# A two-piece first copy, smaller first weight loads, another warm-up and another assumed landing time in a self-scheduling attention and MLP kernel

## The chip, the cores and the metric

The kernel runs on one core of a Trainium2 chip. The metric is the device time of one execution in microseconds (us). Before: 277.12 us, median of three executions (277.1 to 277.2). Several of the runs below were made on another chip or at another time, so each change is compared with executions of the kernel before in the same job, alternating with it on the same chip.

Short names: PE is the matmul engine, ACT, DVE and POOL are the other three compute engines, and SP is the queue that issues all DMAs. "PE idle" in this text is counted from starts: the distance from one matmul's start to the next one's, less the columns streamed at the full rate (a 512-column matmul follows the one before it after 0.216 us, a 320-column one after 0.136 us). The profile's own waits are about 0.17 us shorter, because it records 0.30 us for a 320-column matmul although the next one starts after 0.136 us.

## The reference, cut to what matters

```python
# x: 2048 tokens x 640; 32 heads of 20; MLP width 1536; all bf16
xn = layernorm(x)
q, k, v = split_heads(xn @ wqkv)
phi(u)  = concat(softmax(u @ w_phi), softmax(-(u @ w_phi)))     # per head
kv, z   = phi(k)^T v, sum over tokens of phi(k)
o       = (phi(q) @ kv) / (phi(q) @ z + 1e-6)
return x + o @ wo + (silu(xn @ w1) * (xn @ w3)) @ w2
```

The kernel folds w_phi into the query and key weights first ("the fold"). That needs wk transposed, and a transposing DMA load fetches it.

## The kernel before

The kernel is written for a builder inside the same file. The author gives nine streams of work (layer norm, folds, attention, MLP chunks and so on). The builder keeps a small model of each engine and of the DMA bus, and again and again places the step that the model says could start first. **The model's numbers decide the order of the instructions on the chip.** A wrong number costs nothing by itself, but it may give a worse order, and a corrected one may too.

```python
# in commit(): the model's time at which a DMA has landed
self.bus = max(self.bus, t + 0.5) + o.cost / (280e3 if o.part else 305e3)
o.end = self.bus + (1.6 if t < 3.5 else 2.6)
...
def mm(o, l, r, start, stop, shared=False, cost=None):
    ... cost=max(n / 2400 + 0.003, 0.055) if cost is None else cost
...
def first_loads():
    load_x(0, 1); load_x(1, 2); load_x(2, 3)            # token tiles of 128
    for a in (0, 320):                                  # wv in two halves
        P.dma("SP", wv[:, :, a:a + 320], ...)
    load_x(3, 4)
    w13(0, 512)                                         # w1, w3: first 512 columns = 4 MLP chunks
    P.dma("SP", phi_s[:], phi_t)
    P.dma("SP", wqkT[:, DC:2 * DC, :], A_wqkv[:, D:2 * D], True)   # wk, transposed
    load_x(4, 8); load_x(8, 12)
...
def warm_up():                                          # PE works on zeros until tokens are there
    for _ in range(7):
        mm(bank(7), z[:, 0:128], z, True, True)         # 512 columns
    for n, cols, rep in ((2, 88, 10), (4, 66, 8)):      # 52 small ones, row groups side by side
        ...
def xn_transpose(t, k):                                 # tiles 0 to 3: by PE, then a copy out of PSUM
    for dc in range(DC):
        tr(PSb[...], x_tok[:, t, 128 * dc:128 * dc + 128])
    evac(xnT[:, :, t * 128:(t + 1) * 128], src)         # one copy of 640 columns
...
def loads():                                            # tiles 4 to 15: normalised, then transposed by DMA
    ...  P.dma("SP", xnT[:, :, t * 128:(t + 1) * 128], x_tok[:, t, :], True)
    ...  # after tile 7: w13(512, 1024), load_x(12, 16)
def consts_late():                                      # at the end of the norm stream
    ...
    memset("POOL", v2[...][:, :, :, DH], 1.0)           # the ones beside v, interleaved with v's columns
...
# out_tile(), last tile: (0, 0, 384), (1, 384, D)
```

Until w13(512, 1024) has landed there are four MLP chunks (2.16 us of PE each) that PE can use. And the memset of v's ones writes between v's columns: the builder tracks memory in small pieces and finds both in the same ones, so it makes a v copy that is placed after the memset wait for it.

The softmax here doesn't subtract the row's maximum and nothing guards it: scores larger than these inputs give would overflow.

## Time and profile before

| | before |
|---|---|
| median time | 277.12 us |
| span of the profiled execution | 274.9 us |
| PE busy | 268.9 us |
| PE starts real work (first transposes) | 5.99 us |
| start of the last DVE add | 272.45 us |

Two lines of the page of the kernel before: the span, and each engine's busy time, share and instructions.

```profile
span 274.9 us, 4782 instructions
...
PE 268.9 (98%) x1961; PEld 163.3 (59%) x1961; DVE 181.9 (66%) x318; ACT 108.1 (39%) x197; POOL 60.5 (22%) x93
```

The waits of PE (us in total, how often, the longest in us):

```profile
PE PS L101 <- DVE t L101: 1.3, 1, 1.3
PE PS L101 <- ACT xnT L101: 1.0, 2, 0.8
PE PS L101 <- DVE x_tok L101: 0.6, 1, 0.6
PE PS L101 <- DMA wqkT<-in_A_wqkv_dram: 0.5, 1, 0.5
```

These four are all. The first is the time before anything is in SBUF. The others lie between 5 and 17 us. The opening in order of time (start, length, instruction, count, and in brackets the idle time before it and what ended it):

```profile
5.99 0.45 PE L101 MATMUL PS<-ident,x_tok 128*128 128x128 bf16 x5 [0.57 <-DVE x_tok L101]
6.48 0.70 ACT L101 ACTIVATE xnT<-PS 128x640 bf16<-128x640 bf16 x1 [4.17 <-PE PS L101]
7.24 0.85 PE L101 MATMUL PS<-wv,xnT 128*128 128x320 bf16 x5 [0.80 <-ACT xnT L101]
...
9.39 0.39 DVE L101 TENSOR_SCALAR x_tok<-x_tok,mv,rstd 128x640 bf16<-128x640 bf16 x1
9.90 0.44 PE L101 MATMUL PS<-ident,x_tok 128*128 128x128 bf16 x5
...
14.02 2.32 PE L101 MATMUL PS<-xnT,w_s 128*128 128x512 bf16 x10
16.79 1.76 PE L101 MATMUL PS<-BDc,wqkT 128*128 128x140 bf16 x30 [0.45 <-DMA wqkT<-in_A_wqkv_dram]
```

PE transposes tile 0 at 5.99 us, ACT copies it, the first v matmuls run at 7.24 us. The first MLP chunk runs at 14.02 us, then PE stands until wk's transposed load lands, folds at 16.79 us and runs the second chunk. The fourth chunk of the first 512 columns runs much later, as PE's own timeline shows:

```profile
39.28 2.32 PE L101 MATMUL PS<-xnT,w_s 128*128 128x512 bf16 x10
```

The end: DVE's last add, on the second part (256 columns) of the last tile:

```profile
272.45 0.42 DVE L101 TENSOR_TENSOR xres<-PS,xres 128x256 bf16<-128x256 f32 x1 [1.30 <-PE PS L101]
```

About 2.5 us pass from that add's start to the end.

### The profile page before, as it was taken

What the parts mean: (1) busy time and instruction counts of PE and PEld (TensorE: products, weight loads), DVE (VectorE), ACT (ScalarE), POOL (GpSimd) and SP (SyncE); (2) the same over time, 40 slices, a digit from 0 to 9 for tenths busy, and PEclk for the clock granted to TensorE, in tenths of its full rate; (3) what the DMA queues carried; (4) which work ended last, traced back from release to release, by engine and by line L of the source; (5) the groups of instructions that cost most, each with busy time, mean ns of one, the idle gap of its engine ahead of it and who ended that gap; (6) DMA issues with size and microseconds to landing.
All of it is one profiled execution on the core that took longest, in us unless ns stands there. A gap on an engine that the chain in (4) does not pass through costs nothing.

```text
span 274.9 us, 4782 instructions
## 1 busy us (share of the span) xinstructions
PE 268.9 (98%) x1961; PEld 163.3 (59%) x1961; DVE 181.9 (66%) x318; ACT 108.1 (39%) x197; POOL 60.5 (22%) x93
## 2 busy tenths in 40 slices
PE   6999999999999999999999999999999999999996
PEld 2656666676447555555555455567446777777774
DVE  5459869999764698999899799978963121111112
ACT  2567987987821335445554544411320000000000
POOL 4404493999984100000000000000000000000000
DMA  7971899650000731111112111232300212121211
GB/s 202 296 223 37 176 244 295 115 145 0 0 0 2 222 117 24 25 24 26 24 31 43 24 25 26 49 46 52 93 5 0 89 56 82 61 84 61 81 42 48
DMA packets 40326, 21.96 MB, mean 80 GB/s; under 512 B 26736, under 2 KB 40304, under 8 KB 40304
## 3 DMA queue, kind: packets, MB, share of 16 engines
q1 hardware_dynamic: 40304, 21.66, 31.9%
q8 instruction: 15, 0.25, 0.4%
q14 instruction: 7, 0.06, 0.1%
HBM read 12.81 MB, written 2.62 MB: 56 GB/s over the span
## 4 chain that ended last, share of the span: by engine, by line
PE 81%; DMA 7%; DVE 5%; SPq 2%; ACT 2%; issue 1%; POOL 1%
PE PS L101 81%; DMA wqkT<-in_A_wqkv_dram 4%; DVE bst L101 3%; DMA x_tok<-in_A_x_dram 3%; SPq L113 2%; ACT x_tok L101 1%; DVE mv L101 1%; POOL rstd L101 1%; ACT ekt L101 0%; DVE Wkp L101 0%; DVE hT L101 0%; DVE t L101 0%; ACT v L101 0%; DVE xres L101 0%; DVE x_tok L101 0%
## 5 line engine op out<-in xcount | busy, mean ns | idle before, releaser
L101 PE MATMUL PS<-xnT,w_s 128*128 128x512 bf16 x480 | 107.2, 379 | 0.1
L101 PEld LDWEIGHTS PS<-xnT,w_s 128*128 128x128 bf16 x480 | 46.8, 98 | 55.1 <-ACT Wkp L101 0.3
L101 PE MATMUL PS<-w_s,hT 128*128 128x320 bf16 (+2 forms) x384 | 54.9, 299 | 0.0
L101 DVE TENSOR_TENSOR xres<-PS,xres 128x640 bf16<-128x640 f32 (+2 forms) x17 | 13.4, 786 | 54.0 <-PE PS L101 54.0
L101 ACT ACTIVATE th<-PS 128x512 f32<-128x512 f32 x48 | 28.7, 598 | 46.8 <-PE PS L101 46.8
L101 PEld LDWEIGHTS PS<-w_s,hT 128*128 128x128 bf16 x384 | 37.6, 98 | 14.6
L101 DVE SCALAR_TENSOR_TENSOR t<-th,PS 128x512 bf16<-128x512 f32 x48 | 32.7, 682 | 15.4 <-ACT th L101 15.4
L101 POOL TENSOR_TENSOR ekt<-ekt,rS 128x640 bf16<-128x640 bf16 x32 | 39.4, 1271 | 4.1 <-DVE rS L101 4.1
L101 DVE SCALAR_TENSOR_TENSOR hT<-t,PS 128x512 bf16<-128x512 bf16 x48 | 33.0, 687 | 1.7
L101 PE MATMUL PS<-wv,xnT 128*128 128x320 bf16 x160 | 24.7, 299 | 1.0 <-ACT xnT L101 1.0
L101 ACT ACTIVATE EqT<-PS 128x512 bf16<-128x512 f32 x40 | 21.7, 595 | 9.9 <-PE PS L101 9.9
L101 PE MATMUL PS<-wo_s,oT 128*128 128x320 bf16 (+2 forms) x160 | 24.5, 299 | 0.0
L101 DVE TENSOR_TENSOR prod<-PS,g_s 128x1280 bf16<-128x1280 f32 x16 | 23.9, 1491 | 0.5
L101 PE MATMUL PS<-Wkp,xnT 128*128 128x320 bf16 x160 | 23.9, 299 | 0.1
L101 PE MATMUL PS<-xnT,Wqp 128*128 128x512 bf16 x100 | 23.7, 379 | 0.0
L101 ACT ACTIVATE ekt<-PS 128x640 bf16<-128x640 f32 x32 | 20.8, 717 | 6.0 <-PE PS L101 6.0
L101 DVE TENSOR_REDUCE S<-ekt 128x64 f32<-128x1280 bf16 x16 | 23.0, 1441 | 0.0
L101 PEld LDWEIGHTS PS<-wv,xnT 128*128 128x128 bf16 x160 | 15.2, 98 | 7.5 <-ACT xnT L101 1.5
L101 PEld LDWEIGHTS PS<-Wkp,xnT 128*128 128x128 bf16 x160 | 15.4, 98 | 6.4 <-ACT ekt L101 0.3
L101 PEld LDWEIGHTS PS<-wo_s,oT 128*128 128x128 bf16 x160 | 15.6, 98 | 6.1
L101 DVE BATCH_NORM_STATS2 bst<-x_tok 128x6 f32<-128x320 bf16 x32 | 15.3, 478 | 5.8 <-DMA x_tok<-in_A_x_dram 5.2
L101 ACT ACTIVATE e_s<-PS 128x64 f32<-128x64 f32 x32 | 9.1, 283 | 22.0 <-PE PS L101 21.0
(53 smaller groups left out, 162.4 us busy)
## 6 DMA issues: line engine op xcount, KB each, us to landing
w_s<-in_B_w_dram SPq DMA_DIRECT2D x6, 640.0 KB, 6.7
xres<-in_A_x_dram SPq DMA_DIRECT2D x16, 160.0 KB, 2.4
out_dram<-xres SPq DMA_DIRECT2D x15, 160.0 KB, 1.8
x_tok<-in_A_x_dram SPq DMA_DIRECT2D x3, 640.0 KB, 6.2
w_s<-in_B_w_dram SPq DMA_DIRECT2D x1, 1920.0 KB, 8.0
wv<-in_A_wqkv_dram SPq DMA_DIRECT2D x2, 400.0 KB, 4.6
wo_s<-in_A_wo_dram SPq DMA_DIRECT2D x1, 800.0 KB, 4.7
x_tok<-in_A_x_dram SPq DMA_DIRECT2D x4, 160.0 KB, 2.9
```

What stands on the lines that cost most here:

```text
L101: o = _Op(eng, lambda: m(*args, **kw), r, w, cost)
L113: o = _Op(eng, lambda: m(out, in_), self.regions(in_), self.regions(out), nbytes, True)
```

## The change

Its intent: let the first v matmuls start on a part of the first tile, load the first MLP columns in smaller pieces, tell the builder that wk comes 1 us later so that it puts other work before the fold, make the matmul costs truer, simplify the warm-up, and shorten the last add.

```diff
-                o.end = self.bus + (1.6 if t < 3.5 else 2.6)
+                o.end = self.bus + (1.6 if t < 3.5 else 2.6) + (o.part == "T" and o.cost > 4e5)
...
-             cost=max(n / 2400 + 0.003, 0.055) if cost is None else cost)
+             cost=n / 2400 + 0.0027 if cost is None else cost)
...                                   # tr(): cost 0.06 -> 0.056
-        w13(0, 512)
+        w13(0, 256)
+        w13(256, 512)
...                                   # warm_up()
-        for _ in range(7):
+        for _ in range(9):
             mm(bank(7), z[:, 0:128], z, True, True)
-        for n, cols, rep in ((2, 88, 10), (4, 66, 8)):
-            ...                       # the 52 small matmuls
...                                   # xn_transpose()
-        evac(xnT[:, :, t * 128:(t + 1) * 128], src)
+        if t == 0:
+            copy("ACT", dst[:, 0:2, :], src[:, 0:2, :])
+            copy("ACT", dst[:, 2:DC, :], src[:, 2:DC, :])
+        else:
+            evac(dst, src)
...                                   # out_tile(), last tile
-            for q, lo, hi in ((0, 0, 384), (1, 384, D)):
+            for q, lo, hi in ((0, 0, 512), (1, 512, D)):
```

Only the two large transposed weight loads are over 4e5 bytes, so the extra 1 us touches only them.

More of the change, by code (lines that the diff above doesn't have):

```diff
@@ L349, in mm @@
              dict(start=start, stop=stop, skip_group_check=shared),
-             cost=max(n / 2400 + 0.003, 0.055) if cost is None else cost)
+             cost=n / 2400 + 0.0027 if cost is None else cost)
     def tr(o, i, idn=None):
         idn = ident[:] if idn is None else idn
-        P.op("PE", "transpose", [o], [i, idn], (o, i, idn), cost=0.06)
+        P.op("PE", "transpose", [o], [i, idn], (o, i, idn), cost=0.056)
     def free(ap):
@@ L467, in warm_up @@
         memset("DVE", z, 0.0)
-        for _ in range(7):
+        for _ in range(9):
             mm(bank(7), z[:, 0:128], z, True, True)
-        for n, cols, rep in ((2, 88, 10), (4, 66, 8)):
-            r = 128 // n
-            for _ in range(rep):
-                for i in range(n):
-                    mm(bank(i, cols), z[r * i:r * i + r, 0:128], z[r * i:r * i + r, 0:cols], True, True,
-                       cost=0.05 / n)
     def xn_transpose(t, k):
@@ L481, in xn_transpose @@
         src = PSb[:, k * 1024:k * 1024 + D].rearrange("p (c n) -> p c n", n=128)
-        evac(xnT[:, :, t * 128:(t + 1) * 128], src)
+        dst = xnT[:, :, t * 128:(t + 1) * 128]
+        if t == 0:
[3 more added lines that the diff above has]
+            evac(dst, src)
     def block_diag():
```

## The prediction

> **What bounds the kernel now.** TensorE. The page gives PE 268.9 us busy of a 274.9 us span; the list of waits has only 3.6 us of PE waits, all in the first 17 us: 1.3 us (nothing loaded yet), 0.57 us for the first normalised token tile, 0.8 and 0.17 us for an ACT copy of a transposed tile, and 0.45 us for the transposed wk weights. From 17 to 272.45 us the timeline shows PE without a gap worth naming. About 2.5 us follow PE's last start (DVE add 0.42 us, store about 1.5 us). So the change can gain only in the opening gaps and in the tail: at most about 2 us, under 1%.
>
> **What the change does.**
>
> 1. First tile's copy in two pieces. ACT takes 0.70 us for 640 columns and 0.44 us for 320, so by that line (an estimate) 0.39 and 0.49 us for 256 and 384. The first two matmuls of the tile need only the first piece; the last three start about 0.15 us earlier. The next transposes are bound by DVE (tile 2 is normalised at 9.78 us, PE transposes it at 9.90), so I keep only 0.07 us.
>
> 2. wk transpose assumed later, by 1 us. This changes only the order in which the kernel's builder places work. PE now does one MLP chunk (14.02 to 16.2 us), stands until 16.79 us for wk's transposed load, folds wk, then does the next chunk. I expect two chunks (2.16 us each) before the fold; PE then reaches it near 18.3 us. Gain: the 0.45 us wait plus the drain, 0.6 us.
>
> 3. 256-column loads. Two more DMA issues (0.43 to 0.9 us each on the SP queue) and 512-byte rows. wk's transpose is issued at about 7.5 us, not 6.25, and lands 0.5 to 1.3 us later, at 17.2 to 18.0 us. Point 2 hides that. The load of tokens 4 to 7 (issued at 13.18 us) slips by about 1 us too; PE has one spare MLP chunk (run at 39.28 us before) to cover it. No gain by itself.
>
> 4. Warm-up: nine full matmuls instead of seven and 52 small ones. It ends near 5.2 us, not 5.42, so the gap before 5.99 us grows at no cost, if the clock stays up. The Trainium skill ("TensorE: Matmul & The Clock Gate", Part 1) says that the array runs at half rate until one window of about 3.4 us has been busy; here the warm-up matmuls are 0.43 us apart and the transposes at 5.99 us 0.056 us apart, so it agrees. I give 8% to a cold start.
>
> 5. Last tile 512 and 128. PE time is equal: at 128 columns the transposes go 0.056 us apart with a weight load each (the same page, "Back-to-back issue gap", says about 81 ns; this trace is faster). The last add shrinks from 0.42 to about 0.29 us (estimate from 0.82, 0.56 and 0.42 us for 640, 384 and 256 columns). The store has 256-byte rows; I expect the same 1.5 us. Gain 0.13 us.
>
> 6. Matmul costs in the builder become truer; the order may shift anywhere, worth plus or minus 0.3 us.
>
> Sum: 0.07 + 0.6 + 0.13 = 0.8 us: 276.3 us, range 275.6 to 277.1. Faster by over 2%: 0.01; within 2%: 0.97; slower: 0.02.
>
> **Shown right by:** no PE wait for wk's load and two MLP chunks before the fold; two ACT copies for tile 0; last add 0.29 us. **Shown wrong by:** PE still waiting for wk, the first real matmuls over 0.2 us apart, or new PE waits between 20 and 50 us for token tiles.
>
> **What would break it:** wk landing after 18.3 us, later token loads starving PE, or a cold clock.

## The result, and the profile after

The changed kernel took 277.65 us (median of six, 277.08 to 278.49); the kernel before, in the same job, 277.16 us (six, 277.02 to 277.33). The ratio is 1.002, with a 95% interval of 1.0004 to 1.0036. Ratios here are the mean time of one kernel's fast runs over that of the other's of the same rounds, so not quite the ratio of the medians quoted. The predicted 276.3 us and its range (to 277.1) were missed: a small gain was forecast and a small loss came.

The profiled execution is the fastest of the six. The same two lines of its page:

```profile
span 275.4 us, 4682 instructions
...
PE 269.4 (98%) x1911; PEld 161.9 (59%) x1911; DVE 182.0 (66%) x319; ACT 107.0 (39%) x197; POOL 60.5 (22%) x93
```

PE is as full as before, but 0.5 us more of it. PE's waits:

```profile
PE PS L101 <- DVE t L101: 1.3, 1, 1.3
PE PS L101 <- DVE x_tok L101: 1.0, 2, 0.6
PE PS L101 <- ACT xnT L101: 0.5, 1, 0.5
PE PS L101 <- ACT v L101: 0.3, 1, 0.3
PE PS L101 <- DMA xnT<-x_tok: 0.3, 1, 0.3
PE PS L101 <- ACT Wkp L101: 0.2, 1, 0.2
```

The wait for wk is gone. Three small ones have come: for ACT's copy of v, for a token tile's DMA transpose, and for a copy within the fold. The opening:

```profile
5.90 0.46 PE L101 MATMUL PS<-ident,x_tok 128*128 128x128 bf16 x5 [0.59 <-DVE x_tok L101]
6.39 0.76 ACT L101 ACTIVATE xnT<-PS 128x256 bf16<-128x256 bf16 x2 [4.09 <-PE PS L101]
6.83 0.96 PE L101 MATMUL PS<-wv,xnT 128*128 128x320 bf16 x5 [0.48 <-ACT xnT L101]
...
9.69 0.39 DVE L101 TENSOR_SCALAR x_tok<-x_tok,mv,rstd 128x640 bf16<-128x640 bf16 x1
10.14 0.45 PE L101 MATMUL PS<-ident,x_tok 128*128 128x128 bf16 x5 [0.37 <-DVE x_tok L101]
...
14.27 4.48 PE L101 MATMUL PS<-xnT,w_s 128*128 128x512 bf16 x20
18.58 1.11 PE L101 MATMUL PS<-BDc,wqkT 128*128 128x140 bf16 x18
...
28.09 2.32 PE L101 MATMUL PS<-xnT,w_s 128*128 128x512 bf16 x10
```

Two MLP chunks (20 matmuls) now stand before the fold, as predicted; the fold starts at 18.58 us with no wait for wk. All four chunks are used up by 30.25 us: the fourth, which ran at 39.28 us before, now runs at 28.09 us. The later fold delays more than itself. Tiles 4 and later are normalised, then transposed by DMA. ACT normalises tile 4 after the two exponentials of the first key tile (`ekt`), and these wait for PE's key matmuls, which follow the fold. ACT before (first two lines) and after:

```profile
22.38 1.30 ACT L101 ACTIVATE ekt<-PS 128x640 bf16<-128x640 f32 x2 [1.84 <-PE PS L101]
23.57 1.73 ACT L101 ACTIVATE x_tok<-x_tok,rstd 128x640 bf16<-128x640 bf16 x2
24.21 1.30 ACT L101 ACTIVATE ekt<-PS 128x640 bf16<-128x640 f32 x2 [1.54 <-PE PS L101]
25.40 1.73 ACT L101 ACTIVATE x_tok<-x_tok,rstd 128x640 bf16<-128x640 bf16 x2
```

So the first DMA transpose of a token tile is issued at 26.35 us, not 24.51. In all 16 profiles of fast executions it is issued 7.72 to 7.76 us after the fold starts. PE further on, at the two new waits:

```profile
39.76 1.52 PE L101 MATMUL PS<-wv,xnT 128*128 128x320 bf16 x10
41.56 1.52 PE L101 MATMUL PS<-Wkp,xnT 128*128 128x320 bf16 x10 [0.28 <-DMA xnT<-x_tok]
...
56.02 1.52 PE L101 MATMUL PS<-wv,xnT 128*128 128x320 bf16 x10
57.85 0.49 PE L101 MATMUL PS<-BDc,wqkT 128*128 128x140 bf16 x6 [0.32 <-ACT v L101]
```

The ten matmuls at 39.76 us need 1.36 us; the next start is 1.80 us later, so PE idles 0.44 us, for tile 8: its DMA transpose landed at 41.43 us, before at 40.80, when PE was still at its fourth chunk. Likewise 0.47 us before 57.85 us. What held the second, as ACT's and POOL's timelines show it (ACT's v copy, then POOL's memset of v's ones):

```profile
57.09 0.71 ACT L101 ACTIVATE v<-PS 128x640 bf16<-128x640 f32 x1 [2.61 <-POOL v L101]
54.62 2.37 POOL L101 MEMSET v<- 128x512 bf16 x1
```

The memset ends at 56.99 us and the copy starts at 57.09 us. In the kernel before, the same memset ran at 82.1 us, after all v copies. The end:

```profile
273.09 0.29 DVE L101 TENSOR_TENSOR xres<-PS,xres 128x128 bf16<-128x128 f32 x1 [0.26 <-PE PS L101]
```

The last add takes 0.29 us, not 0.42.

Counted from PE's first transposes (5.99 and 5.90 us) to PE's last matmul (272.14 and 272.84 us), the changed kernel needs 0.79 us more. From PE's starts, before against after:

| stretch | PE idle before | PE idle after | difference |
|---|---|---|---|
| first transposes to first MLP chunk (whole length 8.03, 8.37) | | | +0.34 |
| before the fold | 0.61 | 0 | -0.61 |
| in and just after the fold | 0.27 | 0.33 | +0.06 |
| near 41 us (token tile) | 0 | 0.45 | +0.45 |
| near 50 and 57 us (v copy, fold of the queries) | 0.24 | 0.75 | +0.51 |
| sum | | | +0.75 |

After that nothing more is won or lost: at 78 us ACT's instructions come 0.63 us later than before, and DVE's last add 0.64 us.

### The profile page after: what moved, and what is told of

It reads as the page before. It is cut to its first block, busy times and chain, and to the rows that moved or that the text cites. A ratio compares the mean times of both kernels' runs of the same rounds, so it can differ in the third digit from the quotient of the medians.

```text
span 275.4 us, 4682 instructions
## 1 busy us (share of the span) xinstructions
PE 269.4 (98%) x1911; PEld 161.9 (59%) x1911; DVE 182.0 (66%) x319; ACT 107.0 (39%) x197; POOL 60.5 (22%) x93
## 4 chain that ended last, share of the span: by engine, by line
PE 83%; DVE 5%; DMA 5%; POOL 3%; SPq 2%; issue 1%; ACT 1%; POOLq 0%; ACTq 0%
PE PS L101 83%; DMA x_tok<-in_A_x_dram 5%; DVE bst L101 3%; POOL ekt L101 2%; SPq L113 2%; POOL v L101 1%; DVE mv L101 1%; DVE S L101 1%; POOL eps L101 0%; ACT Wkp L101 0%; ACT v L101 0%; DVE hT L101 0%; DVE t L101 0%; DVE x_tok L101 0%; ACT Wqp L101 0%
## 5 line engine op out<-in xcount | busy, mean ns | idle before, releaser
L101 DVE BATCH_NORM_STATS2 bst<-x_tok 128x6 f32<-128x320 bf16 x32 | 15.3, 478 | 4.5 <-DMA x_tok<-in_A_x_dram 3.9
```

The costliest lines, as they stand in the source:

```text
L101: o = _Op(eng, lambda: m(*args, **kw), r, w, cost)
```

## The experiments

First theory ("the order"): what the reordering saves before the fold is lost again at 41 and 57 us. Rivals: the smaller loads cost; the new warm-up starts the clock late in some executions, which would explain the spread of 1.4 us. A third theory, the instruction refill, came from the first four runs.

Every edit is against the kernel before or the changed one, as said. I compared the instruction order of each edited kernel with that of its base. The two-piece copy, the small loads and the tail leave the order of PE, DVE and POOL as it is; the later wk alone decides the number of chunks before the fold and the place of the memset. The new warm-up changes the PE order only after 90 us. The traces show that such late changes of order cost nothing: the lead of that run over the kernel before is 0.70 us at 64 us and 0.69 us at the last add, and that of the changed kernel without the later wk (below) 0.74 us at both.

### One part alone on the kernel before

**Two-piece copy** (edit: the `xn_transpose` hunk).

> The kernel before with the first tile's copy in two pieces, and nothing else; the order of work on PE, DVE and POOL stays as before. If the copy is only a small local gain, as predicted, the first v matmul starts about 0.35 us earlier and the whole runs 0.1 to 0.3 us faster. If DVE's order (statistics of tile 3, which wait for their load, ahead of tile 2's normalisation) swallows it, under 0.1 us is left: PE stands longer before the transposes of tile 2.

Measured: 276.8 us against 276.71, ratio 0.9994 (0.9958 to 1.0031). Too wide to see 0.1 us. The profiled execution was an unlucky one in two ways: the first half of wv landed at 7.28 us instead of 6.34, which alone held the first v matmul to 7.41 us; and the array's clock fell back to half for one stretch. The profile by windows (length, busy us of each engine, then the clock as PEclk, DMA share, GB/s):

```profile
core 0: us, PE busy (x) PEld busy (x) DVE busy (x) ACT busy (x) POOL busy (x), PEclk, DMA share, GB/s
7.50:10.90 3.40, 3.40 (x17) 2.14 (x17) 1.51 (x4) 1.30 (x3) 0.95 (x3) 0.50 1.08 352
10.90:13.00 2.10, 2.10 (x20) 1.42 (x19) 0.84 (x2) 1.17 (x3) 0.48 (x1) 0.99 1.37 151
```

In that stretch 320-column matmuls started 0.267 us apart, not 0.136. So the part alone is inconclusive in time. That it moves the wait is seen in the changed kernel: first v matmul at 6.83 us, but 0.53 us of PE idle before tile 2's transposes, which there was none of before; tile 2's normalisation (9.69 us) stands behind tile 3's statistics on DVE.

**Small loads** (edit: the `w13` hunk), run twice.

> The kernel before with the first MLP columns in four 256-column loads instead of two of 512; the order of all engines stays as before. Loads theory: the wk transpose lands 0.5 to 2 us later, so PE's wait before the fold grows from 0.6 us to 1.1 to 2.6 us, tile 3 lands about 0.3 us later, and the run is 0.5 to 2 us slower, with a wider spread. Rival (the loads are harmless, the lost time is the order's): within 0.2 us of before.

Measured: 278.0 us against 276.71, ratio 1.003 (0.9994 to 1.0066). All six executions lie above 277.3. The profile had a cold clock until 10.47 us, so it could not say why.

> The small loads alone once more. Refill theory: the instruction packet falls between 12 and 15 us, amid the loads of w1, w3 or wk; wk lands at 16.7 us or later, PE stands 0.4 us or more before the fold, and the median is again 0.5 to 1.4 us above before. Rival (the first run was an unlucky chain of late clock starts): within 0.3 us of before.

Measured: 277.31 us against 276.8, ratio 1.0022 (1.0009 to 1.0035). With the clock up, wk landed at 17.09 us and PE idled 0.96 us before the fold. The instruction packet of the refill theory came at 12.4 us. So the small loads on the old warm-up do cost, here 0.5 us.

**New warm-up** (edit: the `warm_up` hunk).

> The kernel before with nine full warm-up matmuls in place of seven and 52 small ones. Warm-up theory: in some executions the clock is released later, so the median rises by about 0.5 us and the spread from 0.3 to over 1 us, as the changed kernel shows. Rival: no difference over 0.1 us and a spread of about 0.3 us.

Measured: 276.03 us against 276.71, ratio 0.9973 (0.9939 to 1.0008). Five of the 11 executions of before exceed 276.8, and two of this one's six; its four best lie at 275.9 to 276.06. So neither expectation held: it is 0.7 us **faster** in the medians, but the interval includes 1, so the times alone do not show it. Its trace shows no wait for wk at all: wk landed at 15.17 us, not 16.66.

**Later wk** (edit: the first hunk).

> The kernel before, but its builder assumes the two large transposes 1 us later; two MLP chunks then stand before the fold, and the POOL memset of v's ones moves to before the last v copies. Order theory: the 0.6 us wait for wk goes, but 0.3 to 0.5 us of PE idle come back near 41 us (a token tile's transpose, no MLP chunk left as filler) and about 0.5 us near 57 us (ACT's v copy waits for the memset): from 0.2 us faster to 0.4 us slower in all. If the order is not to blame, it runs 0.5 to 0.6 us faster.

Measured: 277.74 us against 276.71, ratio 1.0032 (0.9998 to 1.0067). The waits of PE in this profile that before does not have:

```profile
PE PS L101 <- DMA xnT<-x_tok: 0.7, 1, 0.7
PE PS L101 <- ACT v L101: 0.6, 1, 0.6
PE PS L101 <- ACT Wkp L101: 0.2, 1, 0.2
```

This one number in the model brings all three new waits of the changed kernel. Counted from starts, PE idles 0.86 us at 41 us and 0.76 us at 58 us. The order theory expected at most 0.4 us of loss; the medians say 1.0 us (the interval just includes 1).

### Why the new warm-up makes wk land earlier

Where the 52 small matmuls had been, 50 matmuls and as many weight loads are missing. The trace has, besides the data queue, a queue of kind "instruction": 15 packets of 16,384 bytes, spread over the whole span, one for every 124 matmuls on average (93 to 164). The 3,922 PE instructions in the profile of the kernel before, at the 64 bytes that the Trainium skill gives for one ("TensorE: Matmul & The Clock Gate", Part 2, step 2), make 15.3 such packets. The skill's page "Runtime: NRT & Kernel Launch", section "Instruction fetch mechanics", says that each engine's instruction store is refilled by DMA in blocks of 16 KiB, 256 instructions, and that the cost is mostly hidden. The size agrees. For PE itself it is hidden too: PE has no idle time at the later packets, at 28.11 and 61.02 us for example. The guess was that the packet holds up data that the DMA engines move at the same time.

Kernel before, DMA queues from 14.4 to 15.6 us (packets, MB, share; the data queue's line is left out), then the view of the transposed weight's tile: the load's time from issue (at 6.25 us) to landing, and PE's wait for it.

```profile
q8 instruction: 1, 0.02, 5.8%
DMA to landing us min/median/max: 10.4/10.4/10.4
  PE PS L101: 0.5, 1
```

Kernel before with the new warm-up, the same two views (load issued at 6.34 us); the data queue is the only one in this window. Its first instruction packet comes at 18.88 us, when wk has long landed, and PE has no wait for wk:

```profile
q1 hardware_dynamic: 225, 0.16, 81.9%
DMA to landing us min/median/max: 8.8/8.8/8.8
```

In all profiles of kernels with the old warm-up and 512-column loads (four, with the tail run below) the packet falls at 14.4 to 15.2 us, and wk lands 4.3 us after the small phi load ahead of it in the queue. In the nine where it falls later (from 18.7 us), wk lands 2.7 to 2.8 us after phi. (In the two with the old warm-up and small loads it falls before wk; see below.) To test this rather than argue it, I put 50 tiny matmuls back where PE stands idle anyway:

```diff
 # kernel before with the new warm-up; xn_transpose(), after tile 0's transposes
+        if t == 0:
+            z = t1[:, 2, :]
+            for n, cols, rep in ((2, 88, 9), (4, 66, 8)):
+                ...                   # 18 + 32 matmuls on zeros, into banks 4 to 7
```

> The kernel before with nine warm-up matmuls (the run that was 0.7 us faster) and 50 tiny matmuls on zeros put back, but in PE's idle stretch after the first tile's transposes (6.2 to 7.2 us), where they cost PE nothing. Refill theory: what delayed wk before was one 16 KB packet of PE's own instructions, at 14.4 us, amid wk's transposed load; with nearly as many PE instructions as before it falls there again, wk lands 4.3 us after the small phi load instead of 2.7, near 16.7 us, and PE again stands 0.3 to 0.7 us before the fold. Rival (nine full matmuls help by an earlier clock): wk lands near 15.3 us and PE does not wait for it.

Measured: 276.8 us against 276.68, ratio 1.001 (0.9989 to 1.0031): no gain over before is left, though this interval overlaps that of the new warm-up alone. The same two views, the queues from 14.7 to 16 us:

```profile
q8 instruction: 1, 0.02, 5.3%
DMA to landing us min/median/max: 10.3/10.3/10.3
  PE PS L101: 0.4, 1
```

The packet is back (14.81 us), wk lands at 17.01 us, 4.30 us after phi, and PE idles 0.53 us before the fold. The refill theory is shown: adding or removing 50 matmuls moves the packet, and wk with it by 1.5 to 1.8 us. The semaphore records of the traces show how. A load's completion is counted in 16 steps. In the kernel before, wk's last data packet ends at 14.65 us; 15 of the 16 steps come by 15.14 us and the last one at 16.66. With the new warm-up the last data packet ends at 14.65 us too, and all 16 steps come by 15.17 us. In all five profiles with the packet amid wk, one step alone is late, 2.19 to 2.25 us after the packet's start; the packet itself takes 1.05 to 1.11 us. So one of the 16 steps is held up, not the bulk of the data. Why that step comes another 1.1 to 1.2 us after the packet's end is not shown.

The small loads with the new warm-up:

> The small loads with the nine-matmul warm-up. Refill theory: the packet falls at about 19 us, wk lands at 15.6 to 16.2 us, PE waits at most 0.2 us for it, and the median is 0.3 to 0.8 us under before, as with the nine-matmul warm-up alone. Rival (the loads cost by themselves): 0.3 to 1 us above before.

Measured: 276.46 us against 276.8, ratio 0.9991 (0.9975 to 1.0008); packet at 18.93 us, wk landed at 15.75 us, no wait for wk. So the small loads are slow only together with the old warm-up: the packet then delayed the last of the four loads (in the repeat it landed 2.7 us after the third, where the others are 1.1 us apart), and wk after it.

### Parts of the changed kernel

> The changed kernel once more, beside the three below on one chip. If the order is what costs, the trace again has no PE wait for wk, two MLP chunks before the fold, and PE idle of 0.4 to 0.9 us near 41 us (a token tile's transpose) and of 0.5 to 0.8 us near 57 us (ACT's v copy behind the POOL memset). Median 0 to 1.2 us above before; spread over 0.5 us if loads and clock start vary.

Measured: 276.77 to 278.43 us in five executions against 277.08, ratio 1.0018 (0.9998 to 1.0038). The sixth, the profiled one, took 406.49 us at a granted clock of 0.658; it is not used, so the expected waits could not be checked here. The times agree with the first result.

**Memset late.** Edit on the changed kernel:

```diff
+        while done["n"] < T - 1:
+            yield None
         yield consts_late
```

> The changed kernel with the POOL memset of v's ones put late (after the 15th key tile's normalisation), where the kernel before has it; the PE order up to the key-value sums stays as in the changed kernel. Order theory: the idle near 57 us (0.5 to 0.8 us) goes and the run is 0.4 to 0.8 us faster than the changed kernel; the idle near 41 us stays. Rival (the time goes elsewhere, PE only waits later): under 0.2 us.

Measured: 276.73 us, ratio to before 0.9992 (0.9977 to 1.0008), beside 1.0018 for the changed kernel in the same job: 0.26%, or 0.7 us, as expected, though the two intervals overlap. The idle time at 57 us is gone, that at 41 us (0.60 us here) is not, although the clock started late in the profiled execution. In the trace the order theory's second half holds.

**An extra chunk at hand.** Edit, on top of the memset: w13(512, 640) after tile 5, the rest after tile 7.

> As the run before it, and 128 more columns of w1 and w3 are loaded earlier (after token tile 5's transpose is issued), so that one more MLP chunk is at hand near 41 us. If the chunk moved ahead of the fold was PE's filler for 41 us, the idle there goes, and the run is 0.4 to 0.8 us faster than the one with the late memset alone. If the builder does not place the chunk there (its PE order came out the same), or the extra loads delay the token transposes, the idle stays and nothing is gained.

Measured: 277.55 us, ratio 1.0011 (0.9991 to 1.003). A miss: the builder put no chunk there, and the two extra loads stand before the token transposes on the SP queue (tile 8's issued at 35.44 us instead of 34.12), so PE's idle time at 41 us grew from 0.60 to 1.11 us. It shows what PE waits for at 41 us, but not that a chunk there would cure it; that stays open.

**Without the later wk.** Edit: the first hunk undone in the changed kernel.

> The changed kernel without the assumption that wk lands 1 us later: one MLP chunk before the fold, the memset late by the builder's own choice. If the reordering is what costs, the waits near 41 and 57 us go (0.9 to 1.4 us of PE idle) and a wait for wk of at most 0.6 us comes, since wk lands at 15.7 to 16.2 us and PE reaches the fold near 16.4: 0.3 to 1.0 us faster than the changed kernel. If the later wk was needed, PE stands over 0.6 us before the fold.

Measured: 276.28 us against 276.68, ratio 0.998 (0.9963 to 0.9998). All waits of PE:

```profile
PE PS L101 <- DVE t L101: 1.3, 1, 1.3
PE PS L101 <- ACT xnT L101: 0.6, 2, 0.5
PE PS L101 <- DVE x_tok L101: 0.6, 1, 0.6
PE PS L101 <- ACT Wkp L101: 0.2, 1, 0.2
```

No wait for wk, although only one chunk stands before the fold: wk landed at 15.79 us and PE came at 16.24. No wait for a token tile or for v. Two groups remain (275.66 to 275.87 and 276.69 to 276.8). Against the changed kernel's 1.0018 and 1.002 (other jobs, each beside the kernel before) this is 0.4%, about 1.1 us, from one number of the model. It is the deciding run.

**With 512-column loads.** Edit: the `w13` hunk undone in the changed kernel.

> The changed kernel with its first MLP columns in two 512-column loads again; the order of all engines stays. If the four smaller loads cost (the wk transpose issued at 6.3 instead of 9.4 us, tokens 4 to 7 landing 0.2 to 0.8 us earlier), the run is 0.2 to 0.6 us faster than the changed kernel and the wait near 41 us shrinks. Rival: no difference, since the wait near 41 us follows from the order.

Measured: 277.32 us against 276.68, ratio 1.0024 (1.0005 to 1.0043): no gain. The waits of 0.3 us for v and for a token tile are there as in the changed kernel. With the new warm-up the loads are harmless.

### The tail alone

> The kernel before with the last tile split 512 and 128 alone. The last add takes 0.29 us, not 0.42, and the store of 256-byte rows about as long as before: 0.1 to 0.15 us faster, which the spread of such runs may hide. If short rows write slower, the time from the last add to the end grows from 2.0 us and the gain is gone.

Measured: 276.93 us against 276.8, ratio 1.0003 (0.9989 to 1.0018), so 0.13 us cannot be seen in the time. In the profile the last add takes 0.29 us, and from its end to the end of the span pass 2.0 us, beside 2.06 before. The Trainium skill ("DMA: Bandwidth & Descriptors", Specifications) asks for 512 bytes and more for full rate; rows of 256 bytes showed no penalty in this small store (32 KB instead of 64, so shorter rows and less data are not told apart).

### A version without the two harmful pieces

> The kernel before with the nine-matmul warm-up, the two-piece copy and the 512 and 128 tail, without the later wk and without the 256-column loads. If these three parts are the good ones, it is 0.4 to 1.0 us faster than before: the last add takes 0.29 us, not 0.42, and the first v matmul starts 0.35 us earlier. If the warm-up's gain in its own run was chance, 0.1 to 0.3 us.

Measured: 276.71 us against 277.08, ratio 0.9985 (0.9969 to 1.0002), again in two groups (275.93, 275.96, then 276.69 to 277.08). The profiled one, 275.93 us, shows the add of 0.29 us and the first v matmul at 6.85 us.

The groups led to the last edit, which keeps PE busier while the clock decides: on that kernel, ten warm-up matmuls, and two more in the idle stretch after the first transposes.

```diff
-        for _ in range(9):
+        for _ in range(10):
 # xn_transpose(), after tile 0's transposes
+        if t == 0:
+            z = t1[:, 2, :]
+            for _ in range(2):
+                mm(bank(7, 256), z[:, 0:128], z[:, 0:256], True, True)
```

> A version meant to beat both: the kernel before with ten full warm-up matmuls, two 256-column matmuls on zeros in the idle stretch after the first transposes, the two-piece copy and the 512 and 128 tail; no later wk, no 256-column loads. If late clock release makes the spread, no execution is over 0.6 us above the fastest, and the median is 0.7 to 1.2 us under before. If the clock still starts late in some executions, two groups about 1 us apart stay.

Measured: 275.74 us (five, 275.47 to 275.79) against 276.68, ratio 0.9959 (0.9946 to 0.9972). It beats the kernel before, beside which it ran, and by its ratio the changed one too; its spread is 0.3 us. In its profile PE waits for no DMA: after the first 1.3 us only 0.5 us for the first normalised tile and 0.4 us for ACT's copies are left. Since several parts came together here, the run does not say how much of the gain each one has.

## Why the prediction was wrong

**The bound** was right. PE limits, and everything that was won or lost is PE idle time between 6 and 60 us plus the tail. The ceiling of 1% held too.

**Point 2, the step that failed.** The prediction put it: "Gain: the 0.45 us wait plus the drain, 0.6 us." The two chunks before the fold and the missing wait came exactly so. What failed is counting them as a gain. First, PE's stock of filler is four chunks until new columns are loaded, and the token tiles are supplied from the fold on: their first DMA transpose follows its start by 7.7 us. A chunk moved ahead of the fold starts that supply later (26.35 us, not 24.51) and no longer stands between the fold and tile 8 to cover it. Tile 8 lands 0.63 us later, PE comes to it 0.32 us earlier (at 41.12 us, before at 41.44), and PE idles 0.45 us. I had read the fourth chunk at 39.28 us as a "spare" that could cover a later token load, and spent it twice. Second, the same number moved the memset of v's ones from 82.1 to 54.6 us, ahead of the last v copies, for 0.48 us. With the later wk on the kernel before, both waits appear; taken out of the changed kernel, both vanish and the time falls by 0.4%. How much of the wait at 41 us is due to the spent chunk and how much to the later tile was not tested apart; only the later wk as a whole was.

Third, the wait was not wk's own lateness. A refill packet of PE's instructions delayed it by 1.5 us, and dropping the small warm-up matmuls in the same change moved that packet out of the way. So the reordering worked around a wait that another line of the diff had removed.

**Point 3** had the direction wrong. wk was issued even later than predicted (9.37 us, not 7.5), but landed at 15.96 us, earlier than before, not at 17.2 to 18.0. "No gain by itself" was right in the changed kernel (1.0024 without them, 1.0018 and 1.002 with); on the old warm-up they cost 0.5 us or more.

**Point 4** was wrong about value: "at no cost" hid a gain through the refill, the 0.61 us of PE idle time before the fold. The chance of a cold start, 8%, was too low. Four of the 16 profiled fast executions ran their first v matmuls at half rate, two with each warm-up. It is not the difference between the two kernels, whose profiles both have the full clock there. It makes part of the spread: in these four profiles the first MLP chunk starts at 15.3 to 15.7 us, in the other 12 at 14.0 to 14.7. The five executions of the filled warm-up lie within 0.3 us; only one of them has a trace, so that a late clock is cured is likely, not shown.

**Point 1** was right in mechanism and beyond measurement in size. **Point 5** was right: 0.29 us, no slower store. **Point 6** allowed 0.3 us for shifts of order, as noise from the matmul costs; the shift that counted came from point 2. The changed kernel without the later wk still has the new costs, and its lead over the kernel before does not change from 64 us to the end.

The 0.34 us lost in the opening is not explained by the change: DVE could take up tile 3 at 8.51 us in this execution and at 8.21 before. Over all profiles tile 3 lands at 8.2 to 9.4 us with the old warm-up and at 8.2 to 8.7 with nine or ten full matmuls, with either load size. What sets it is open.

## What to carry to other kernels

When PE is full but for one wait, work moved into that wait leaves a hole where it came from; before counting a gain, ask what PE will run at the old place, and whether a model's number moves anything else in the order. Before working around a late load, look at what else the DMA engines carry at that time: here the instruction stream itself did it, and dropping 50 useless matmuls removed the wait that the reordering only moved. Change such numbers one at a time, since two changes of one diff here cured the same wait, and one of them cost 1.1 us.

## What the Trainium skill lacked or had wrong

- "Runtime: NRT & Kernel Launch", Instruction fetch mechanics: it calls the refill mostly hidden. For PE it is; but the 16,384-byte packet at 14.45 us delayed a transposed load in flight by about 1.5 us (landing 4.3 instead of 2.7 to 2.8 us after the load ahead of it). No page that I found says or sizes how an instruction refill delays a data load.
- "CRC Debugging" (under "Comparing the Two Runs") puts the instruction-refill DMAs on queue 14. In this trace the 15 instruction packets that recur about every 124 matmuls are on queue 8; queue 14 carries seven more of 8,192 bytes, whose engine the trace does not name. So queue 14 is not the whole list.
- "TensorE: Matmul & The Clock Gate", Back-to-back issue gap: it gives about 81 ns for a 128-column matmul with its weight load in a stream. Here such pairs start 56 ns apart (five transposes, and all 17 matmuls of the last 128 columns).
- The same page, Part 1, on the clock: it says that the same kernel is released earlier or later from run to run, and that agrees (the kernel with the small loads alone was at half rate until 10.47 us in one profile and until 6.32 in the other; two more profiles show 10.27). Its table has the clock fall back after an idle window of about 3.4 us; here one execution fell back to half rate from 7.5 to 10.9 us after being released at 4.09 us, with PE idle for about 2.1 us of the 3.4 us before. So a partly busy window was enough. The page tells of such a case in another kernel, with short idle stretches, but gives no share of idle time at which it happens.
